# A gated recurrence with a mixture of adapters: the adapter weights issued from GpSimd instead of the sync engine

## The chip, the cores and the metric

The kernel runs on one core of a Trainium2 chip. The metric is the device time of one execution in microseconds (us), the median of several runs. A profile of one execution gives the span from the first to the last instruction; it is a little shorter than the measured time.

A core has TensorE (PE in the profile, with the loads of its stationary operand as PEld), VectorE (DVE), ScalarE (ACT), GpSimd (POOL) and a sync engine (SP) that does no arithmetic and here issues transfers. Each engine works through its own instructions in order; semaphores join them.

## The reference

For each of 4 batches and 8 heads, a recurrence over 768 steps with a 48 x 48 state, then a mixture of 8 low-rank adapters over all 3072 rows of width 384, of which each row uses two:

```python
for t in range(S):                       # S = 768, D = 48
    state = alpha[:, :, t, :, None] * state + np.einsum('bhd,bhe->bhde', k[:, :, t], v[:, :, t])
    y[:, :, t] = np.einsum('bhd,bhde->bhe', q[:, :, t], state)
...
x = y.transpose(0, 2, 1, 3).reshape(B * S, H * D)      # 3072 x 384
logits = x @ w_gate                                    # 8 experts
topk = np.argpartition(-logits, 2, axis=1)[:, :2]
w = softmax over the two chosen logits
delta[mask] += w[mask, k, None] * ((x[mask] @ A[e]) @ B[e])   # rank 16
return x + delta
```

The inputs are q, k, v, alpha of 4.7 MB each, and the small weights w_gate (384 x 8), A (8 x 384 x 16) and B (8 x 16 x 384). The output has 4.7 MB.

## The kernel before

The 768 steps of a batch are cut into 6 chunks of 128, so that there are 24 units (batch, chunk). Within a unit all 8 heads are handled together, and the recurrence becomes matrix products over a chunk plus a state carried from chunk to chunk. The stages of a unit, by the names that the code gives its functions and tiles:

- `ld` loads a whole batch of one input into a tile of 128 partitions (`a_t`, `k_t`, `q_t`, `v_t`, each 1.2 MB, two buffers each by `TURNS`).
- `ln` (ScalarE) takes the logarithm of alpha for two chunks at once into `lg`; `cum` (TensorE) forms its running sums; `eup`, `edn`, `edec` (ScalarE) take exponentials of them into `up`, `dn` and `dec`.
- `kgm`, `qgm`, `vbc` (GpSimd) multiply k by `up` into `kg`, q by `dn` into `qg`, and cast v into `vb`.
- `tr` (TensorE) transposes `kg` and `qg`; `kq` (VectorE) copies the transposes out of PSUM; `at` (TensorE) multiplies them; `msk` (VectorE) applies the causal mask into `at_sb`.
- `kv` (TensorE) and `sdm` (VectorE) carry the state, `sdec`.
- `yt` (TensorE) forms the transposed result, `xs` (ScalarE) copies it, `z` (TensorE) multiplies it by `W`, which holds A and w_gate side by side; `gmx`, `gdf`, `gex`, `gwu`, `grd`, `gzw` (VectorE, and ScalarE for the exponential) choose and weigh the two experts.
- `zt`, `qs`, `av`, `delta` (TensorE) build the output of the unit in one PSUM bank `y`, with `B_all` as the last factor; `fin` (ScalarE) copies it to `o`, and `st` stores it.

The order of all this on each engine is fixed when the kernel is built, by a planner. `graph` makes a node for each stage of each unit, with an assumed cost from `STAGES` and a priority that is the unit's number less a lead from `LEAD`; `CHAINS` and `RINGS` give the dependencies, the latter those from buffers being used again. `list_order` then places the nodes one after another on their engines, and `plan` returns them in that order; `emit` calls the function of each. The stores are placed behind the last load.

The loads stand in the order of `load_list`: alpha, k, q, v of batch 0, then an item `"w"`, which is all the weights, then the twelve loads of batches 1 to 3. All of them are issued by the sync engine (`load_engine`), so that they are in one queue. The item `"w"` is `wload`: for each half of the 128 partitions (even and odd heads of a pair, rows 0 to 47 and 64 to 111) four transfers of A, one for each pair of heads, and one of w_gate, and one transfer of B at the end; eleven in all, into the float32 tiles `W_st` and `B_st`. `wcast` then casts these on VectorE into the bfloat16 tiles `W` and `B_all`, with two copies for the halves of W and one for B:

```python
nc.vector.tensor_copy(out=W[rows], in_=W_st[rows])
...
nc.vector.tensor_copy(out=B_all, in_=B_st)
```

For the planner this cast is a node `wcast`, on which every `z` depends.

Of the kernel before, what the change touches and what calls it, by code (L numbers as in the profile page):

```python
# [13 lines left out]
F4 = mybir.dt.float32  # L14

B, H, S, D = 4, 8, 768, 48
# [3 lines left out]
E = 8  # L20
R = 16
P = 128
NP = H // 2
HP = 64
NW = E * R + E
G = 2
RING = 4
QRING = 3
VRING = 5
SRING = 4  # L30
# [8 lines left out]
def _bc_mid(src: bass.AP, reps) -> bass.AP:  # L39
# [17 lines left out]
    "st": ("DMA", 655, 2455),  # L57
}
LEAD = {
    "vld": 4.5, "vbc": -39.07, "ln": -78.94, "cum": -6.57, "edn": -64.56, "eup": 56.94,  # L60
    "edec": -16.31, "kgm": -144.25, "qgm": -36.9, "tr": 10.78, "kq": -190.71, "sdm": -68.3,
    "kv": 0.43, "at": 71.13, "msk": -50, "qs": 15.22, "av": 80.82, "xb": 0.5, "xt": 0.4,
    "xs": -65.35, "z": -58.98, "zc": -33.57, "gmx": -40, "gdf": 13.75, "gex": 14.25, "gwu": -45.2,
    "grd": 9.49, "gw": -7.12, "gzw": -43.82, "yt": -51.21, "zt": -11.39, "zs": -8.95,
    "delta": 56.73, "fin": -111.57, "st": 100,
}
CHAINS = (
    "ln cum eup kgm tr kq at msk yt xs z gmx gdf gex gwu grd gzw zt zs delta fin st",
# [1 line left out]
    "vbc yt", "zt qs av delta", "zt av",  # L70
)
RINGS = (
    ("kgm", "eup", 3), ("qgm", "edn", 3), ("sdm", "edec", 6), ("tr", "kgm", RING), ("kv", "kgm", RING),
    ("tr", "qgm", QRING), ("kv", "vbc", VRING), ("av", "vbc", VRING), ("at", "kq", 5), ("av", "kq", 5),
    ("msk", "at", 1), ("av", "msk", 4), ("z", "xs", 3), ("delta", "zs", 3), ("st", "fin", 24),
    ("qs", "sdm", SRING), ("kv", "sdm", 1), ("kgm", "cum", 3), ("qgm", "cum", 3), ("at", "tr", 5),
    ("av", "tr", 5), ("z", "yt", 3), ("delta", "zt", 3), ("st", "zt", 24),
    ("edec", "kv", -1), ("qs", "kv", SRING - 1), ("delta", "gzw", 3),
)
HOLDS = {  # L80
# [81 lines left out]
def load_list():  # L162
    out = []
    for b in range(B):
        if b in ():
            seq = [(0, 0)]
            for c in range(NCH):
                seq += [(1, c), (2, c), (0, c + 1), (3, c)]
            out += [(b, i, c) for i, c in seq if c < NCH]
        else:  # L170
            out += [(b, i, None) for i in range(4)]
    return out[:4] + ["w"] + out[4:]


def load_engine(x):
    return "ACT" if x in ((0, 1, 0), (0, 3, 0)) else "SP"


def graph(lead):
    nodes, deps = {}, []  # L180

    def has(f, u):
        c = u % NCH
        if not 0 <= u < NU or (f in ("sdm", "edec", "qs") and c == 0):
            return False
        if f == "ln" and u // NCH not in () and u % G:
            return False
        return not (f == "kv" and c == NCH - 1)

    def dep(a, b):  # L190
        if a in nodes and b in nodes:
            deps.append((a, b))

    for f in STAGES:
        for u in range(NU):
            if f != "ln2" and has(f, u):
                t = STAGES["ln2" if f == "ln" and u // NCH not in () else f]
                nodes[f, u] = t + (u - lead[f],)
    nodes["wcast", 0] = ("DVE", 700, 700, 0)
    dep(("wcast", 0), ("z", 0))  # L200
    for u in range(NU):
        for line in CHAINS:
            names = line.split()
            for f, g in zip(names, names[1:]):
                dep((f, u if has(f, u) or f != "ln" else u - 1), (g, u))
        for f, g, d in RINGS:
            dep((f, u - d), (g, u))
        dep(("kv", u - 1), ("sdm", u))
        for w in range(NU):
            if w // G == u // G - 2:  # L210
                dep(("cum", w), ("ln", u))
    for x, item in enumerate(load_list()):
        n = ("ld", x)
        eng = load_engine(item)
        if item == "w":
            nodes[n] = ("DMA", 4000, 5300, x)
            dep(n, ("wcast", 0))
            continue
        b, i, c = item
        t = 1060 if c is not None else 4450  # L220
        nodes[n] = ("DMB" if eng == "POOL" else "DMA", t, t + 1300, x)
        mine = [(READER[i], b * NCH + k) for k in (range(NCH) if c is None else (c,))]
        for m in mine:
            dep(n, m)
        if eng == "POOL":
            nodes["is", x] = ("POOL", 1000, 1000, b * NCH + (c or 0) - 6)
            deps.append((("is", x), n))
            n = ("is", x)
        if b >= TURNS[i]:
            for k in range(NCH):  # L230
                dep((READER[i], (b - TURNS[i]) * NCH + k), n)
    last = ("ld", len(load_list()) - 1 - 0)
    for u in range(NU):
        dep(last, ("st", u))
    holds = {}
    for f, readers in HOLDS.items():
        for u in range(NU):
            if (f, u) in nodes:
                holds[f, u] = [(g, u + d) for g, d in readers if (g, u + d) in nodes]
    return nodes, deps, holds  # L240
# [22 lines left out]
def kernel(  # L263
# [11 lines left out]
    nc = tc.nc  # L275
# [2 lines left out]
    loads = ctx.enter_context(tc.tile_pool(name="loads", bufs=3))  # L278
    outp = ctx.enter_context(tc.tile_pool(name="outp", bufs=24))
    consts = ctx.enter_context(tc.tile_pool(name="consts", bufs=1))  # L280
    scal = ctx.enter_context(tc.tile_pool(name="scal", bufs=3))
    trsb = ctx.enter_context(tc.tile_pool(name="trsb", bufs=5))
    atsb = ctx.enter_context(tc.tile_pool(name="atsb", bufs=4))
    moep = ctx.enter_context(tc.tile_pool(name="moep", bufs=3))
    PS = bass.MemoryType.PSUM
    ps_s = ctx.enter_context(tc.tile_pool(name="ps_s", bufs=1, space=PS))
# [13 lines left out]
    ENG = {"SP": nc.sync, "ACT": nc.scalar, "POOL": nc.gpsimd}  # L300

    def load(b, i, c, eng):
        name, src = SRC[i]
        if raw[b][i] is None:
            raw[b][i] = loads.tile([P, H * NCH, 64], F4, name=name, tag=name, bufs=TURNS[i])
            batches[b][i] = raw[b][i].rearrange("p (h c) d -> p c h d", h=H)[:, :, :, 0:D]
        if c is None:
            eng.dma_start(  # L308
                out=raw[b][i][:, :, 0:D], in_=src[b].rearrange("h (c j) d -> j (h c) d", j=C))
        else:  # L310
            eng.dma_start(
                out=batches[b][i][:, c],
                in_=src[b][:, c * C:(c + 1) * C, :].rearrange("h j d -> j h d"))

    W_st = consts.tile([P, NP, NW], F4, name="W_st")
    B_st = consts.tile([P, DM], F4, name="B_st")
    W = consts.tile([P, NP, NW], F2, name="W")
    B_all = consts.tile([P, DM], F2, name="B_all")

    def wload():  # L320
        for hh in range(2):
            rows = slice(HP * hh, HP * hh + D)
            for p in range(NP):
                f0 = (2 * p + hh) * D
                nc.sync.dma_start(  # L325
                    out=W_st[rows, p, 0:E * R].rearrange("f (e r) -> f e r", e=E),
                    in_=moe_A[:, f0:f0 + D, :].rearrange("e f r -> f e r"))
            nc.sync.dma_start(
                out=W_st[rows, :, E * R:NW],
                in_=moe_w_gate.rearrange("(p t f) e -> t f p e", p=NP, t=2)[hh])  # L330
        nc.sync.dma_start(out=B_st, in_=moe_B.rearrange("e r f -> (e r) f"))

    def wcast(_):
        for hh in range(2):
            rows = slice(HP * hh, HP * hh + D)
            nc.vector.tensor_copy(out=W[rows], in_=W_st[rows])  # L336
        nc.vector.tensor_copy(out=B_all, in_=B_st)

    items = load_list()

    def ld(x):
        if items[x] == "w":
            wload()
        else:
            load(*items[x], ENG[load_engine(items[x])])

    order = plan()[1]
    early = [n for n in order if n[0] == "ld"][:4]
    for n in early:
        ld(n[1])  # L350
# [5 lines left out]
        out=suf, in_=suf, compare_op=ALU.is_gt, fill=0.0, base=0,  # L356
# [14 lines left out]
    for i in range(2):  # L371
        t = consts.tile([P, G, H, HP], F2, name=f"lg{i}")
        nc.gpsimd.memset(t[:, :, :, D:HP], 0.0)
        lgs.append(t)
    for lst, nm, n in ((kgs, "kg", RING), (qgs, "qg", QRING), (vbs, "vb", VRING)):
        for i in range(n):
# [3 lines left out]
    for i in range(SRING):  # L380
# [8 lines left out]
        out=mask, in_=mask, compare_op=ALU.is_ge, fill=0.0, base=0,  # L389
# [4 lines left out]
    st = [dict() for _ in range(NU)]  # L394
# [46 lines left out]
    def kgm(u):  # L441
        s = st[u]
        b, c = units[u]
        s["kg"] = kgs[u % RING]
        nc.gpsimd.tensor_tensor(  # L445
# [178 lines left out]
    def store(u):  # L624
# [2 lines left out]
        nc.sync.dma_start(out=out[t0:t0 + C, :], in_=st[u]["o"])  # L627

    emit = dict(
        ld=ld, wcast=wcast, ln=ln, cum=cum, eup=eup, edn=edn, edec=edec, kgm=kgm, qgm=qgm, vbc=vbc,  # L630
        tr=tr, kq=kq, sdm=sdm, kv=kv, at=at, msk=msk, qs=qs, av=av, yt=yt, xs=xs, z=z,
        gmx=gmx, gdf=gdf, gex=gex, gwu=gwu, grd=grd, gzw=gzw, zt=zt, zs=zs, delta=delta, fin=fin,
        st=store)
# [33 lines left out]
```

## Time and profile before

| | before |
|---|---|
| measured time, median of 3 (lowest, highest) | 111.11 us (111.11, 111.3) |
| span of the profiled execution | 110.4 us |
| mean granted TensorE clock | 0.956 of full speed |
| TensorE busy | 79.6 us (72%) |
| VectorE busy | 76.0 us (69%) |
| ScalarE busy | 64.3 us (58%) |
| GpSimd busy | 61.9 us (56%) |
| moved by the DMA engines | 24.21 MB, 219 GB/s on average |

In the lines of the profile, `out<-in` names the tiles by the program's names, a line number such as L325 is one of the kernel's code, and `xN` counts instructions. The idle time before a group and what ended it stand at the end of a line. SPq is the time in which the sync engine's queue issues transfers; a transfer moves on after its issue, so its landing has to be read from those that wait for it. Busy times of engines overlap each other and do not add up to the span.

### The profile page before, as it was taken

The numbers are of one execution on the slowest core, as the hardware profiler recorded it, in microseconds if no ns is written. First come the engines' busy times: TensorE is split into PE (matmuls) and PEld (weight loads), VectorE is DVE, ScalarE is ACT, GpSimd is POOL, SyncE is SP. The second block draws the span as 40 slices with busy tenths as digits, with TensorE's granted clock in tenths as the row PEclk, the third lists the DMA queues.
The fourth block names the chain that finished last, engine by engine and source line by source line (L and its number), as shares of the span: only waits on it lengthen the run. The fifth ranks groups of instructions, "written<-read, shape, count | busy, mean of one in ns | idle before, by whom it ended". The sixth has DMA issues, their size and how long they took to land.

```text
span 110.4 us, 3341 instructions
## 1 busy us (share of the span) xinstructions
PE 79.6 (72%) x1312; PEld 61.0 (55%) x1312; DVE 76.0 (69%) x227; ACT 64.3 (58%) x177; POOL 61.9 (56%) x97
## 2 busy tenths in 40 slices
PE   0005206981896959988599999999939998997850
PEld 0003105761775747876486777776727976865720
DVE  4000002989976597799797979999947699999810
ACT  4029402542028997693979559967955367563560
POOL 7600649999001185899575949983749749500000
PEclk9999999999769999999999999999996799999995
DMA  0979899533889898996979989785959899441052
GB/s 19 307 219 297 236 281 291 96 35 83 222 230 296 214 299 242 250 287 187 320 229 278 283 236 290 198 243 146 286 143 308 324 391 356 145 175 39 6 207 78
DMA packets 32064, 24.21 MB, mean 219 GB/s; under 512 B 4272, under 2 KB 32048, under 8 KB 32048
## 3 DMA queue, kind: packets, MB, share of 16 engines
q1 hardware_dynamic: 32048, 24.00, 73.8%
q8 instruction: 10, 0.16, 0.6%
q14 instruction: 6, 0.05, 0.1%
HBM read 19.28 MB, written 4.72 MB: 217 GB/s over the span
## 4 chain that ended last, share of the span: by engine, by line
SPq 30%; DMA 27%; PE 22%; ACT 11%; issue 3%; DVE 3%; POOL 1%; ACTq 0%
SPq L308 21%; DMA a_t<-in_alpha_dram 16%; DMA q_t<-in_q_dram 11%; SPq L325 8%; PE tr L477 4%; ACT xs L539 4%; PE y L615 3%; ACT lg L402 3%; PE at L507 2%; PE yt L531 2%; PE yt L526 2%; PE y L554 2%; PE z L562 2%; ACT o L622 1%; ACT up L426 1%
## 5 line engine op out<-in xcount | busy, mean ns | idle before, releaser
L445 POOL TENSOR_TENSOR kg<-k_t,up 128x384 bf16<-128x384 f32 x24 | 23.9, 1011 | 14.6 <-DMA k_t<-in_k_dram 9.9
L515 DVE TENSOR_TENSOR at_sb<-at,mask 128x1024 bf16<-128x1024 f32 x24 | 29.2, 1217 | 4.1 <-PE at L507 3.9
L483 DVE COPY kq<-tr 128x1024 bf16<-128x1024 bf16 x24 | 16.2, 683 | 19.5 <-PE tr L477 19.3
L452 POOL TENSOR_TENSOR qg<-q_t,dn 128x384 bf16<-128x384 f32 x24 | 23.6, 1001 | 6.4 <-DMA q_t<-in_q_dram 6.1
L459 POOL CAST vb<-v_t 128x384 bf16<-128x384 f32 x24 | 11.6, 508 | 12.7 <-PE y L554 10.4
L539 ACT CAST xs<-yt 128x512 bf16<-128x512 f32 x24 | 14.2, 599 | 6.6 <-PE yt L531 6.4
L426 ACT ACTIVATE up<-cum 128x384 f32<-128x384 f32 x24 | 11.1, 492 | 9.2 <-PE cum L417 9.0
L411 PE MATMUL cum<-lg,suf 128*128 128x384 bf16 x24 | 8.6, 368 | 8.7 <-ACT lg L402 8.7
L622 ACT COPY o<-y 128x384 f32<-128x384 f32 x24 | 11.4, 481 | 5.3 <-PE y L615 5.3
L477 PE MATMUL tr<-ident,qg 128*128 128x128 bf16 x96 | 10.6, 241 | 5.4 <-POOL qg L452 5.4
L402 ACT ACTIVATE lg<-a_t 128x768 bf16<-128x768 f32 x12 | 10.1, 847 | 7.2 <-DMA a_t<-in_alpha_dram 7.2
L477 PE MATMUL tr<-ident,kg 128*128 128x128 bf16 x96 | 10.6, 241 | 3.3 <-POOL kg L445 3.3
L562 PE MATMUL z<-W,xs 128*128 128x136 bf16 x96 | 9.2, 225 | 4.4 <-DVE W L336 2.7
L464 DVE TENSOR_TENSOR sdec<-kv,dec 128x384 bf16<-128x384 f32 x20 | 10.9, 547 | 1.8 <-PE kv L497 1.8
L431 ACT ACTIVATE dn<-cum 128x384 f32<-128x384 f32 x24 | 11.5, 523 | 0.0
L611 ACT CAST zs<-y 128x128 bf16<-128x128 f32 x24 | 6.4, 266 | 7.9 <-PE y L554 7.4
L477 PEld LDWEIGHTS <-qg 128*128 128x128 bf16 x96 | 7.4, 110 | 5.8 <-POOL qg L452 5.8
L531 PE MATMUL yt<-at_sb,vb 128*64 128x128 bf16 x192 | 10.2, 228 | 0.6 <-DVE at_sb L515 0.5
L507 PE MATMUL at<-kq 48*128 48x128 bf16 x192 | 10.2, 229 | 0.5 <-DVE at_sb L515 0.4
L615 PE MATMUL y<-B_all,zs 128*128 128x384 bf16 x24 | 8.0, 341 | 2.3 <-ACT zs L611 1.5
L562 PEld LDWEIGHTS <-xs 128*128 128x128 bf16 x96 | 5.7, 98 | 6.4 <-ACT xs L539 3.5
L477 PEld LDWEIGHTS <-kg 128*128 128x128 bf16 x96 | 6.6, 106 | 4.7 <-POOL kg L445 3.4
(53 smaller groups left out, 148.9 us busy)
## 6 DMA issues: line engine op xcount, KB each, us to landing
out_dram<-o SPq DMA_DIRECT2D x24, 192.0 KB, 2.7
W_st<-in_moe_A_dram SPq DMA_DIRECT2D x8, 24.0 KB, 2.7
B_st<-in_moe_B_dram SPq DMA_DIRECT2D x1, 192.0 KB, 2.4
a_t<-in_alpha_dram SPq DMA_DIRECT2D x4, 0.2 KB, 8.8
k_t<-in_k_dram SPq DMA_DIRECT2D x4, 0.2 KB, 10.7
q_t<-in_q_dram SPq DMA_DIRECT2D x4, 0.2 KB, 9.9
v_t<-in_v_dram SPq DMA_DIRECT2D x4, 0.2 KB, 9.8
W_st<-in_moe_w_gate_dram SPq DMA_DIRECT2D x2, 6.0 KB, 1.9
```

What stands on the lines that cost most here:

```text
L308: eng.dma_start(out=raw[b][i][:, :, 0:D], in_=src[b].rearrange("h (c j) d -> j (h c) d", j=C))
L402: nc.scalar.activation(lgs[(u // G) % 2][:, :, :, 0:D], batches[b][0][:, c:c + G], AF.Ln)
L445: nc.gpsimd.tensor_tensor(out=s["kg"][:, :, 0:D], in0=batches[b][1][:, c], in1=s["up"], op=ALU.mult)
L452: nc.gpsimd.tensor_tensor(out=s["qg"][:, :, 0:D], in0=batches[b][2][:, c], in1=s["dn"], op=ALU.mult)
L477: nc.tensor.transpose(t[:, w, p, :], pair(src, p), ident[:, :])
L483: nc.vector.tensor_copy(out=s["kq"], in_=s["tr"])
L507: nc.tensor.matmul(t[:, hh, p, :], s["kq"][rows, 0, p, :], s["kq"][rows, 1, p, :], start=True, stop=True)
L515: nc.vector.tensor_tensor(out=s["at_sb"].rearrange("p a b t -> p (a b) t"), in0=s["at"].rearrange("p a b t -> p (a b) t"), in1=_bc_mid(mas ...
L531: nc.tensor.matmul(s["yt"][HP * hh:HP * hh + HP, p, :], s["vb"][:, 2 * p + hh, :], s["at_sb"][:, hh, p, :], start=(c == 0 and p == 0), sto ...
L539: nc.scalar.copy(s["xs"], s["yt"])
L562: nc.tensor.matmul(s["z"], s["xs"][:, p, :], W[:, p, :], start=(p == 0), stop=(p == NP - 1))
L622: nc.scalar.copy(s["o"], s["y"])
```

## The change

The weights leave the queue of the sync engine. The item `"w"` is gone from `load_list`, and `wload` is a node of its own on GpSimd, ahead of everything else there. It has five DMAs instead of eleven: for each half of the partitions one of A, with the four pairs of heads and the eight experts merged into one access pattern, and one of w_gate, and one of B. For this the columns of `W_st` are laid out as (expert, pair, rank) with the gate's columns behind them, and `wcast` puts them into their places in W, with two copies for each half and one for B, on VectorE. The node `wcast` now depends on `wload`.

In the order that the planner makes of it, the five casts stand on VectorE directly behind the memsets of the set-up and ahead of the first `kq`. In the kernel before they stand behind the third `at_sb`.

With this, five kinds of buffers get one more: `kg` (`RING` 4 to 5), `up` and `dn` (the pool `scal` 3 to 4), `kq` (the pool `trsb` 5 to 6) and `at_sb` (the pool `atsb` 4 to 5), with the numbers in `RINGS` to match, and `LEAD` has new values, which change the order of the work on all engines. On ScalarE, for one, `dn` now mostly comes ahead of `up`. The copy of the transposes, `kq`, is a VectorE instruction in both kernels.

```diff
-RING = 4
+RING = 5
...
-    return out[:4] + ["w"] + out[4:]
+    return out
...
-    nodes["wcast", 0] = ("DVE", 700, 700, 0)
+    nodes["wload", 0] = ("POOL", 8000, 13000, -99)
+    nodes["wcast", 0] = ("DVE", 1600, 1700, 99)
+    dep(("wload", 0), ("wcast", 0))
...
-    scal = ctx.enter_context(tc.tile_pool(name="scal", bufs=3))
-    trsb = ctx.enter_context(tc.tile_pool(name="trsb", bufs=5))
-    atsb = ctx.enter_context(tc.tile_pool(name="atsb", bufs=4))
+    scal = ctx.enter_context(tc.tile_pool(name="scal", bufs=4))
+    trsb = ctx.enter_context(tc.tile_pool(name="trsb", bufs=6))
+    atsb = ctx.enter_context(tc.tile_pool(name="atsb", bufs=5))
...
-    W_st = consts.tile([P, NP, NW], F4, name="W_st")
+    W_st = consts.tile([P, NP * NW], F4, name="W_st")
...
-    def wload():
+    def wload(_):
         for hh in range(2):
             rows = slice(HP * hh, HP * hh + D)
-            for p in range(NP):
-                f0 = (2 * p + hh) * D
-                nc.sync.dma_start(
-                    out=W_st[rows, p, 0:E * R].rearrange("f (e r) -> f e r", e=E),
-                    in_=moe_A[:, f0:f0 + D, :].rearrange("e f r -> f e r"))
-            nc.sync.dma_start(
-                out=W_st[rows, :, E * R:NW],
+            nc.gpsimd.dma_start(
+                out=W_st[rows, 0:E * NP * R].rearrange("f (x r) -> f x r", r=R),
+                in_=bass.AP(tensor=moe_A.tensor, offset=moe_A.offset + hh * D * R,
+                            ap=[[R, D], [2 * D * R, E * NP], [1, R]]))
+            nc.gpsimd.dma_start(
+                out=W_st[rows, E * NP * R:].rearrange("f (p e) -> f p e", p=NP),
                 in_=moe_w_gate.rearrange("(p t f) e -> t f p e", p=NP, t=2)[hh])
-        nc.sync.dma_start(out=B_st, in_=moe_B.rearrange("e r f -> (e r) f"))
+        nc.gpsimd.dma_start(out=B_st, in_=moe_B.rearrange("e r f -> (e r) f"))
 
     def wcast(_):
         for hh in range(2):
             rows = slice(HP * hh, HP * hh + D)
-            nc.vector.tensor_copy(out=W[rows], in_=W_st[rows])
-        nc.vector.tensor_copy(out=B_all, in_=B_st)
+            nc.vector.tensor_copy(
+                W[rows, :, 0:E * R].rearrange("f p (e r) -> f e p r", e=E),
+                W_st[rows, 0:E * NP * R].rearrange("f (e p r) -> f e p r", e=E, p=NP))
+            nc.vector.tensor_copy(
+                W[rows, :, E * R:NW], W_st[rows, E * NP * R:].rearrange("f (p e) -> f p e", p=NP))
+        nc.vector.tensor_copy(B_all, B_st)
```

## The prediction

> **What bounds the kernel now.** I read four views of the kernel before, in this order: the chain of work that ended last, the sync engine's queue in order of time, the busy time of the engines by stretches, and the waits. The chain first, since it says what kind of thing the end hangs on:
>
> ```profile
> SPq 30%; DMA 27%; PE 22%; ACT 11%; issue 3%; DVE 3%; POOL 1%; ACTq 0%
> SPq L308 21%; DMA a_t<-in_alpha_dram 16%; DMA q_t<-in_q_dram 11%; SPq L325 8%; PE tr L477 4%; ACT xs L539 4%; PE y L615 3%; ACT lg L402 3%; PE at L507 2%; PE yt L531 2%; PE yt L526 2%; PE y L554 2%; PE z L562 2%; ACT o L622 1%; ACT up L426 1%
> ```
>
> SPq is the queue that issues the loads, DMA the flight of a load. Together they are 57% of the chain: the end hangs on when the big loads arrive, and 8% (8.8 us of 110.4) is one line, L325, the small weight loads. The queue in order of time (start, duration, then the transfer) shows where those sit:
>
> ```profile
> 11.14 3.89 SPq L308 DMA_DIRECT2D v_t<-in_v_dram  x1
> 15.08 5.84 SPq L325 DMA_DIRECT2D W_st<-in_moe_A_dram  x4
> ...
> 21.48 3.28 SPq L325 DMA_DIRECT2D W_st<-in_moe_A_dram  x4
> ...
> 25.32 0.44 SPq L331 DMA_DIRECT2D B_st<-in_moe_B_dram  x1
> 25.97 0.70 SPq L308 DMA_DIRECT2D a_t<-in_alpha_dram  x1
> 27.12 4.85 SPq L308 DMA_DIRECT2D k_t<-in_k_dram  x1
> ```
>
> The last load of batch 0 is issued by 15.03, the first of batch 1 only at 25.97: eleven small issues hold the queue for 10.9 us, some 4 us of which is waiting behind the loads already queued (the first of L325 takes 4.29), the rest 0.44 to 0.47 us each and one of 1.76. The stretches (after the length: busy time of PE, PEld, DVE, ACT, POOL with counts, the granted clock, the DMA engines' busy share, GB/s) show what this does to the transfers:
>
> ```profile
> 16.00:20.00 4.00, 2.49 (x27) 1.93 (x28) 1.23 (x2) 0.94 (x3) 3.54 (x4) 1.00 0.95 284
> 20.00:22.00 2.00, 2.00 (x26) 1.65 (x27) 1.89 (x3) 1.09 (x4) 2.00 (x4) 1.00 0.49 53
> 22.00:24.00 2.00, 1.74 (x36) 1.30 (x30) 1.71 (x3) 1.33 (x4) 2.00 (x4) 1.00 0.44 47
> 24.00:26.00 2.00, 1.15 (x21) 0.84 (x18) 2.00 (x4) 0.64 (x2) 2.00 (x4) 1.00 0.18 16
> ```
>
> From 20 to 26 us the DMA engines are busy 0.98 + 0.88 + 0.36 = 2.2 us of 6 and move next to nothing. The waits (engine, line, released by: total us, times, longest) and VectorE in order of time show who pays:
>
> ```profile
> DVE kq L483 <- PE tr L477: 19.3, 5, 15.8
> POOL kg L445 <- DMA k_t<-in_k_dram: 9.9, 2, 7.4
> PE z L562 <- DVE W L336: 2.7, 1, 2.7
> ```
>
> ```profile
> 18.16 0.69 DVE L483 COPY kq<-tr 128x1024 bf16<-128x1024 bf16 x1 [15.81 <-PE tr L477]
> ...
> 25.74 0.97 DVE L336 CAST W<-W_st 48x544 bf16<-48x544 f32 x1
> 26.90 0.96 DVE L336 CAST W<-W_st 48x544 bf16<-48x544 f32 x1 [0.20 <-DMA W_st<-in_moe_w_gate_dram]
> 27.89 0.36 DVE L337 CAST B_all<-B_st 128x384 bf16<-128x384 f32 x1
> ...
> 44.65 1.43 DVE L483 COPY kq<-tr 128x1024 bf16<-128x1024 bf16 x2 [0.66 <-PE tr L477]
> ...
> 83.13 0.69 DVE L483 COPY kq<-tr 128x1024 bf16<-128x1024 bf16 x1 [1.69 <-PE tr L477]
> ```
>
> VectorE starts real work at 18.16 and is busy for 76.0 us in all, 1.2 of it before. From 18.2 on, its idle time is about 12 us before its work ends near 105. Some 3.7 us of that lie between 34 and 46 (8.29 us busy of 12), where batch 1 has not arrived, and 3.3 between 78 and 90 (8.70 of 12), around the late q_t and v_t of batch 3. Elsewhere it runs at 94 to 98% (66 to 78 us: 11.7 of 12). So there are two bounds close together: late loads, and behind them VectorE, with TensorE (79.6 us busy) near it.
>
> [...] what the weights cost is 10.9 us of queue, but only 2.2 us of engine time, so only the first can vanish. [...] The trace has no GpSimd DMA at all.
>
> **The change part by part.**
> - *Weight loads leave the sync queue.* The load of a_t of batch 1 can be issued at 15.08 instead of 25.97. It then waits for room as the first weight load does (4.29). Landings follow each other at about 4.45 us when nothing is between (k_t to q_t of batch 1: consumers at 38.16 and 42.61). v_t of batch 0 lands at about 20.8 and a_t of batch 1 at 33.3, 12.5 us apart, so 8.0 us are the gap. The weights' 2.2 to 2.4 us of engine time do not vanish: they move among the loads of batch 0. Net: every load from batch 1 on lands about 5.6 us earlier, q_t of batch 3 at 76.0 instead of 81.6. The buffers allow it: k_t of batch 2, say, would be issued near 40, and its buffer's last reader is done at 27.6.
> - *Five DMAs on GpSimd.* They stand behind the set-up (ending 4.74) and ahead of the first kg, for which GpSimd idles 7.40 us anyway, till 12.14. Behind them are four kg (0.95 apart) and qg, which needs q_t (16.46). [...] I take 8, just hidden.
> - *When the weights land.* The bytes and the 3,456 small rows are the same as before; merged DMAs save issues, not rows. [...] Upper, if packets alternate with those of the loads: (3,456 + 128) / 16 = 224 packets for each DMA engine, each about 10 ns (2.2 us / 224) beside a load packet of about 45 ns (4.4 us for 96): 224 × 55 ns = 12.3, from 5 to 6 us on, so 17.5 to 18.5. I take 18.5, since the queue of the loads is never empty then.
> - *Casts at the head of VectorE.* The order of the changed kernel puts five copies ahead of the first kq, so all of VectorE's work waits for the last weight. Two large copies (48x512 instead of 48x544, at most 0.97), two of 32 columns (about 0.1 each, as the small memsets) and B_all (0.36) are 2.4 us. First kq at 18.5 + 2.4 = 20.9 instead of 18.16: **2.7 us later**. q_t itself may be 2.3 later, which alone would give 20.5, so the two overlap.
> - *Casts leave the middle.* VectorE's 2.5 us from 25.74 to 28.25, and PE's 2.69 wait for W, go: **2.5 us gained**.
> - *Batch 1 is there in time.* q_t at about 37.0 instead of 42.6, while VectorE would come to the end of batch 0's work at about 41: **3.7 us gained**.
> - *Batch 3.* VectorE arrives 3.5 us earlier (2.7 − 2.5 − 3.7), at 81.4 − 3.5 = 77.9; q_t at 76.0 plus 1.0 (qg) and 0.4 (transposes) is 77.5. The wait of 1.69 closes, and about 1.0 of the smaller ones up to 90: **2.7 us gained**.
> - *One more buffer each of kg, up, dn, kq and at_sb, and new leads.* These change the order everywhere; no single row prices that. I count nothing, since VectorE at 94 to 98% in full stretches leaves little to a better order; both signs stay in the range. The transposes' copy stays on VectorE in the code (0.68 each).
>
> Sum: 2.7 − 2.5 − 3.7 − 2.7 = −6.2. Span 110.4 − 6.2 = 104.2; the measured time stands 0.7 above the span (111.1 against 110.4), so **104.9 us**.
>
> **The rivals.**
> - *Better still: VectorE packs tightly.* From 20.9, its remaining 76.0 − 1.2 − 2.3 = 72.5 us at 95%, plus the 4.9 us that follow its last work now: 20.9 + 76.3 + 4.9 = 102.1, so 102.8. For it: stretches of 94 to 98% exist, and buffers get deeper. Against it: the end of the kernel has too few chunks to fill (98 to 106 us: 6.6 of 8).
> - *The earlier loads buy little, and TensorE or the new order becomes the bound.* TensorE is at 3.7 to 3.9 us of 4 in most stretches from 42 on. If only the gap of batch 1 (3.7) is gained and the start's 2.7 against the casts' 2.5 stay: 110.4 − 3.5 = 106.9; with a reshuffle costing another 1 to 2, about 108.5 + 0.7 = 109.
> - *A new wait in place of the old one, slower.* If [...] the weights land at 28, kq starts at 30.4 and everything queued behind it on VectorE shifts: 104.2 + 9.5 + 0.7 = 114.4. GpSimd's kg and qg then wait too. The break-even is a landing near 25. For it: no trace here shows a GpSimd DMA, and an in-order VectorE stands behind it. [...]
>
> **How the numbers follow.** My forecast 0.45, tighter packing 0.22, little gained 0.18, weights late 0.15. All but the last, and a sliver of the third, are faster: faster 0.83, same 0.02, slower 0.15. The range reaches from just under the tight case (101.0) to just under no gain (111.0); it leaves out most of the late case and a very tight one, together about 0.2.
>
> **What would show it.** Right: a_t of batch 1 issued at about 15 and its logarithm near 28; DMA busy share above 0.8 from 16 to 30; the casts ending by 21 and the first kq right after; no wait of VectorE over 1 us between 25 and 90; the DMA share of the chain well under 57%. Wrong: GpSimd's first kg after 16, or casts after 25; a first kq that waits for the casts more than 4 us; batch 1 on time, but VectorE and TensorE with as much idle time as before.

## The result, and the profile after

| | before | after |
|---|---|---|
| measured time, median of 4 (lowest, highest) | 111.17 us (111.11, 111.3) | 108.31 us (106.74, 111.13) |
| ratio after / before, 95% interval | | 0.9635 (0.9573 to 0.9698) |
| span of the profiled execution | 110.4 us | 109.4 us |
| VectorE busy, TensorE busy | 76.0, 79.6 us | 75.3, 77.9 us |
| mean granted TensorE clock | 0.956 | 0.975 |

The changed kernel is faster by 3.65%, which is 4.1 us of 111.17; the medians lie 2.9 us apart. The forecast was 6.2. Ratios here and below leave disturbed runs out, so they are not the quotients of the medians. A second profile of the changed kernel is called "again" below; its span is 107.4 us, 3.0 less than before. None of the profiled executions is a short one: they took 112.17 us (before), 111.13 (after) and 109.18 (again), while the shortest of the changed kernel took 106.7.

The chain of work that ended last, of the kernel after:

```profile
SPq 34%; DMA 29%; PE 13%; POOL 8%; DVE 8%; ACT 3%; issue 3%; ACTq 0%; POOLq 0%
```

The weights' line is gone from it, and yet queue and flight of the loads have 63% where they had 57% (again, 54%): the prediction's sign "well under 57%" did not appear. The sync engine's queue in order of time (start, duration, transfer):

```profile
12.93 5.41 SPq L306 DMA_DIRECT2D v_t<-in_v_dram  x1
18.79 3.83 SPq L306 DMA_DIRECT2D a_t<-in_alpha_dram  x1
23.07 4.31 SPq L306 DMA_DIRECT2D k_t<-in_k_dram  x1
27.82 5.39 SPq L306 DMA_DIRECT2D q_t<-in_q_dram  x1
...
38.18 5.93 SPq L306 DMA_DIRECT2D a_t<-in_alpha_dram  x1
```

a_t of batch 1 is issued at 18.79 instead of 25.97, so the gap of 10.9 us has closed. But v_t of batch 0 is now issued by 18.34 instead of 15.03. GpSimd in order of time shows the new issues, and who waits:

```profile
4.85 1.11 POOL L321 DMA_DIRECT2D W_st<-in_moe_A_dram  x1
...
8.07 0.57 POOL L328 DMA_DIRECT2D B_st<-in_moe_B_dram  x1
16.39 3.86 POOL L443 TENSOR_TENSOR kg<-k_t,up 128x384 bf16<-128x384 f32 x4 [7.75 <-DMA k_t<-in_k_dram]
20.20 3.87 POOL L450 TENSOR_TENSOR qg<-q_t,dn 128x384 bf16<-128x384 f32 x4
```

The five issues run from 4.85 to 8.64, 3.8 us in all. Then GpSimd waits 7.75 us for k_t: the first kg starts at 16.39, where it was 12.14, and the first qg, behind four kg, at 20.20, where it was 16.46. A first kg after 16 is one of the prediction's signs of being wrong; again, it starts at 14.51. VectorE in order of time:

```profile
15.26 0.42 DVE L333 CAST W<-W_st 48x512 bf16<-48x512 f32 x1 [5.15 <-DMA W_st<-in_moe_A_dram]
...
16.05 0.36 DVE L338 CAST B_all<-B_st 128x384 bf16<-128x384 f32 x1 [0.27 <-DMA B_st<-in_moe_B_dram]
21.90 0.69 DVE L481 COPY kq<-tr 128x1024 bf16<-128x1024 bf16 x1 [5.49 <-PE tr L475]
```

The casts are done by 16.4, and then VectorE waits 5.49 us more for the transposes. So the first kq is late (21.90 against 18.16), but not because of the casts. The stretches (length; busy time of PE, PEld, DVE, ACT, POOL; clock; DMA share; GB/s), to be read against those of before:

```profile
16.00:20.00 4.00, 0.61 (x4) 0.34 (x4) 0.36 (x1) 0.00 (x0) 3.61 (x4) 1.00 0.69 198
20.00:22.00 2.00, 0.74 (x6) 0.57 (x7) 0.10 (x1) 0.00 (x0) 2.00 (x3) 1.00 1.00 297
22.00:24.00 2.00, 2.00 (x24) 1.44 (x23) 1.39 (x3) 0.94 (x3) 2.00 (x3) 1.00 0.87 241
24.00:26.00 2.00, 2.00 (x30) 1.82 (x28) 1.89 (x3) 0.94 (x3) 2.00 (x5) 1.00 0.91 272
...
42.00:46.00 4.00, 2.38 (x46) 1.86 (x43) 3.31 (x6) 2.80 (x10) 2.09 (x4) 1.00 0.46 112
```

From 20 to 26 us the DMA engines are busy 5.6 us of 6, where they were 2.2. But from 16 to 20 the core almost stands (PE 0.61 of 4, before 2.49). And a new thin stretch has come in at 42 to 46, at 112 GB/s, under the long issue of a_t that begins at 38.18.

At batch 3, GpSimd and then VectorE:

```profile
78.15 1.96 POOL L450 TENSOR_TENSOR qg<-q_t,dn 128x384 bf16<-128x384 f32 x2 [2.26 <-DMA q_t<-in_q_dram]
```

```profile
79.64 0.69 DVE L481 COPY kq<-tr 128x1024 bf16<-128x1024 bf16 x1 [1.69 <-PE tr L475]
```

q_t of batch 3 is there at 78.15 (again, 77.70), earlier than the 81.64 of before, but later than the 76.0 of the forecast. The wait of 1.69 us at 83.13, which the forecast had closing, has only moved: it is 1.69 us at 79.64 (again, 1.82 at 79.19).

To part the start from the rest I use the time from the first kq to the end of the span: 110.4 − 18.16 = 92.2 us before, 87.5 after and 87.3 again. The start costs 3.7 us (again, 2.0: first kq at 20.13), and the rest gains 4.7 to 4.9. In five experiments below whose GpSimd begins in the same way (e1, e11, e15, e17, e18) the first kq comes at 19.92 to 20.79, so 1.8 to 2.6 us is the usual cost of the start, and 3.7 that of one long execution.

### The profile page after: what moved, and what is told of

Same layout as the page of the kernel before. It is cut to its first block, busy times and chain, and to the rows that moved or that the text cites. A ratio compares the mean times of both kernels' runs of the same rounds, so it can differ in the third digit from the quotient of the medians.

```text
span 109.4 us, 3347 instructions
## 1 busy us (share of the span) xinstructions
PE 77.9 (71%) x1312; PEld 59.2 (54%) x1312; DVE 75.3 (69%) x229; ACT 63.5 (58%) x177; POOL 65.5 (60%) x103
## 4 chain that ended last, share of the span: by engine, by line
SPq 34%; DMA 29%; PE 13%; POOL 8%; DVE 8%; ACT 3%; issue 3%; ACTq 0%; POOLq 0%
SPq L306 34%; DMA v_t<-in_v_dram 20%; DMA q_t<-in_q_dram 10%; POOL vb L457 4%; POOL qg L450 3%; DVE kq L481 2%; DVE at_sb L513 2%; PE tr L475 2%; PE y L613 2%; DVE sdec L462 1%; PE yt L529 1%; PE z L560 1%; PE y L543 1%; PE y L552 1%; PE at L505 1%
## 5 line engine op out<-in xcount | busy, mean ns | idle before, releaser
L475 PE MATMUL tr<-ident,qg 128*128 128x128 bf16 x96 | 10.1, 231 | 4.1 <-POOL qg L450 4.1
L560 PE MATMUL z<-W,xs 128*128 128x136 bf16 x96 | 9.8, 227 | 0.8 <-ACT xs L537 0.6
L475 PEld LDWEIGHTS <-qg 128*128 128x128 bf16 x96 | 6.9, 105 | 4.7 <-POOL qg L450 4.7
L333 DVE CAST W<-W_st 48x512 bf16<-48x512 f32 x2 | 0.8, 422 | 12.3 <-DMA W_st<-in_moe_A_dram 12.3
## 6 DMA issues: line engine op xcount, KB each, us to landing
q_t<-in_q_dram SPq DMA_DIRECT2D x4, 0.2 KB, 10.9
```

What stands on the lines that cost most here:

```text
L475: nc.tensor.transpose(t[:, w, p, :], pair(src, p), ident[:, :])
```

## The experiments

My theory: the gain is the freed queue plus the casts' removal from the middle, less a later start. Rivals: the casts' place is what counts, not the queue; the new leads and buffers bring it; merging eleven DMAs into five would do, from any queue. The runs were made in three groups. The kernel before, beside them, took 113.15 us in the first (110.79 to 113.96), 112.39 in the second (111.04 to 113.66) and 112.48 in the third (110.5 to 113.72), medians of 7; the first group gave no ratio with an interval. Between groups, ratios to the kernel before can be compared, and times only roughly.

### One part alone, planned anew

**Weights on GpSimd alone (e1).** The kernel before with the change's `wload`, `wcast` and nodes, and the old leads and buffers:

```diff
-    return out[:4] + ["w"] + out[4:]
+    return out
...
-    nodes["wcast", 0] = ("DVE", 700, 700, 0)
+    nodes["wload", 0] = ("POOL", 8000, 13000, -99)
+    nodes["wcast", 0] = ("DVE", 1600, 1700, 99)
...
+            nc.gpsimd.dma_start(
```

> The kernel before with the weights issued from GpSimd in five DMAs, and nothing else: its leads and buffer counts are kept. If the gain comes from taking the weights out of the queue of the loads, this run has most of the change's 4.0 us: 106.5 to 108.5. If the new leads and the extra buffers bring it, this run stays within 1 us of 111.2.

Measured: 112.09 us (110.72 to 112.96), no gain outside the spread. Yet the last load was issued by 74.81 instead of 80.29, and the first kq came at 20.03. So the loads were 5.5 us earlier, and the time did not follow.

**Leads and buffers alone (e2).** The kernel after with the weights as before, in eleven DMAs of the sync engine:

```diff
-    return out
+    return out[:4] + ["w"] + out[4:]
...
-            nc.gpsimd.dma_start(
+            for p in range(NP):
...
+                nc.sync.dma_start(
```

> The changed kernel with the weights issued from the sync engine in eleven DMAs as before; the new leads and the extra buffers are kept. If the queue is the cause, this run stays within 1 us of 111.2, with the first load of batch 1 issued near 26. If the order and the buffers are, it has the change's time, about 107.

Measured: 119.46 us (117.82 to 120.63), slower than either theory allowed.

**No weights at all (e6).** The kernel after without the loads of w_gate, A and B; it computes with zero weights:

```diff
     def wload(_):
-        for hh in range(2):
...
+        nc.gpsimd.memset(W_st, 0.0)
+        nc.gpsimd.memset(B_st, 0.0)
```

> The changed kernel with no weight loads at all: GpSimd fills the two staging tiles with zeros, so the adapter part of the result is left out, while all its arithmetic still runs. If the late start of VectorE (21.90 instead of 18.16) is the weights' transfers standing among the loads of batch 0, the first kq is back near 18 to 18.5 and the time is about 3.5 us below the changed kernel's, 103.5 to 104.5. If the four kg ahead of the first qg are the cause, the first kq stays near 21 and the time near 107.

Measured: 106.52 us (104.74 to 108.83), span 103.0. GpSimd, and then VectorE, in order of time:

```profile
12.08 3.86 POOL L435 TENSOR_TENSOR kg<-k_t,up 128x384 bf16<-128x384 f32 x4 [6.33 <-ACT up L416]
```

```profile
17.99 0.69 DVE L473 COPY kq<-tr 128x1024 bf16<-128x1024 bf16 x1 [10.96 <-PE tr L467]
```

kg no longer waits for k_t and is back at 12.08, kq at 17.99: without the weights' transfers the late start is gone. In the kernel after they are under way between 4.85 and about 16 us, as k_t is, with the DMA engines busy throughout (share 1.01 from 4 to 16 us). (The five issues are gone with them, but those ended at 8.64, before k_t had landed.) In the table of DMA queues of the kernel after they take only 2.6% of 109.4 = 2.8 us, as a mean over the DMA engines. The time, though, is 2 to 3 us above the 103.5 to 104.5 that was expected.

**Five merged DMAs on the sync engine (e7),** at the old place in the queue:

```diff
-            nc.gpsimd.dma_start(
+            nc.sync.dma_start(
...
-    return out
+    return out[:4] + ["w"] + out[4:]
```

> The changed kernel with its five merged DMAs issued from the sync engine, between the loads of batch 0 and batch 1, where the eleven stood; leads and buffers of the changed kernel. If the number of issues was the cost and not their engine, the queue is held about 4.3 + 4 x 0.5 = 6.5 us instead of 10.9, batch 1 is issued near 22, the start stays at 18.2, and the time is 106 to 108. If any weight transfer in this queue drains the DMA engines, it is near 110 to 111.

Measured: 114.14 us (111.77 to 115.5), no gain. The five still held the queue from 15.64 to 22.65, 7.0 us for 10.9. The planner made yet another order here, so this doesn't price the 3.9 us saved.

What follows from the group: parts planned anew can't be compared. Each edit changed the order on all engines, and that can move the time by more than the edit: compare e2 with e10, and e1 with e17, below, each beside its own time of the kernel before. So from here the order is held: taken from one of the two kernels, with the items of the weights alone moved by hand.

### One part alone, in a kept order

**The order of after, weights on the sync engine (e10),** behind batch 0 in eleven DMAs, casts just ahead of the first z:

```diff
     for n in early:
         ld(n[1])
+    wload(0)
...
+        if n == ("z", 0):
+            wcast(0)
-        if n not in early:
+        if n not in early and n[0] not in ("wload", "wcast"):
```

> The changed kernel's order on every engine kept as it is, but the weights issued from the sync engine in eleven DMAs behind batch 0, as before, and the casts moved on VectorE to just ahead of the first z. If the queue is what the change gains on, with the order equal, this is 3 to 6 us slower than the changed kernel although its start is 3.7 us earlier: batch 1 issued near 26. If the order alone carries the gain, it is as fast as the changed kernel or faster by its earlier start.

Measured: 113.73 us (113.08 to 115.42), ratio 1.013 (0.9975 to 1.0285). With the weights in the old queue, the new leads and buffers bring nothing. The kernel after in the same group (below) has 0.956 (0.9413 to 0.9706), clear of this interval and 5.6 us less, as the first expectation had it. And nearly the same parts as in e2, in another order, take 5.7 us less, of which 0.8 lies between the two groups.

**The order of before, weights from GpSimd (e11),** the casts at their old place:

```diff
-            wload()
+            pass
...
+    wload(0)
```

> The order of the kernel before kept as it is on every engine, casts included, with only the weights issued from GpSimd in five DMAs at the head. The prediction's arithmetic was made for just this: the loads from batch 1 on 5.6 us earlier and the gaps closed, so 5 us less than before. If an order fits only the arrival times it was planned for, it gains at most 2 us, as the run with old leads and a new plan did.

Measured: 109.5 us (109.1 to 110.18), ratio 0.9799 (0.9697 to 0.99). The queue alone, with the merging of eleven DMAs into five, brings 2.0%, about 2.2 us. The last load was issued by 73.49, 6.8 us earlier than before: more than three times what the time gained. Its chain shows why no more came of it:

```profile
PE 46%; DVE 18%; ACT 13%; DMA 10%; SPq 5%; issue 3%; POOL 1%; ACTq 0%; DVEq 0%; POOLq 0%
```

Queue and flight of the loads are 15% of it, where they were 57%: the loads are no longer what the end hangs on, and TensorE and VectorE are.

**The order of after, casts just ahead of the first z (e15),** weights from GpSimd:

```diff
+        if n == ("z", 0):
+            wcast(0)
-        if n not in early:
+        if n not in early and n[0] != "wcast":
```

> The changed kernel with one thing moved: the five casts stand on VectorE just ahead of the first z instead of at the head. If casts in a stretch where GpSimd multiplies cost 3.7 us, this is 2 to 4 us slower than the changed kernel: ratio to before 0.975 to 0.995. If the cast's place does not matter, 0.955 to 0.965.

Measured: 110.15 us (109.22 to 110.99), ratio 0.984 (0.9675 to 1.0005), against 0.9635 with the casts at the head. VectorE in order of time, and the wait that follows:

```profile
26.54 1.20 DVE L333 CAST W<-W_st 48x512 bf16<-48x512 f32 x1
27.66 0.96 DVE L336 CAST W<-W_st 48x32 bf16<-48x32 f32 x1
28.65 1.17 DVE L333 CAST W<-W_st 48x512 bf16<-48x512 f32 x1
29.74 0.17 DVE L336 CAST W<-W_st 48x32 bf16<-48x32 f32 x1
```

```profile
PE z L560 <- DVE W L336: 3.7, 1, 3.7
```

The same copies that took 0.42 and 0.17 us at the head take up to 1.20 and 0.96 here, and z waits for them. The stretches of this kernel show a second cost:

```profile
26.00:30.00 4.00, 0.33 (x5) 0.21 (x4) 3.94 (x6) 0.50 (x1) 3.13 (x4) 0.95 0.88 241
30.00:34.00 4.00, 4.00 (x41) 2.53 (x40) 3.42 (x12) 1.93 (x4) 0.00 (x0) 0.50 0.57 153
```

While z waits, TensorE is busy for 0.33 us of 4, and in the 4 us after that its clock is 0.50. In the kernel before the wait was 2.69 us, with the same sequel:

```profile
28.50:29.00 0.50, 0.48 (x10) 0.29 (x5) 0.50 (x3) 0.00 (x0) 0.00 (x0) 1.00 1.00 290
29.00:29.50 0.50, 0.47 (x5) 0.35 (x5) 0.50 (x3) 0.21 (x1) 0.00 (x0) 0.61 0.92 247
...
31.50:32.00 0.50, 0.50 (x7) 0.28 (x4) 0.09 (x2) 0.34 (x1) 0.00 (x0) 0.50 0.83 240
...
33.00:34.00 1.00, 0.49 (x5) 0.28 (x4) 1.00 (x3) 0.65 (x1) 0.00 (x0) 1.00 0.91 247
```

For some 3 us the clock is about 0.50. From 22 to 34 us the kernel after has 1.00 throughout.

**The order of before, casts first (e17).** The kernel before with the weights from GpSimd and the casts at the head of VectorE, with the old leads and buffers:

```diff
-            wload()
+            pass
...
+    wload(0)
...
+    wcast(0)
     for n in order:
-        if n not in early:
+        if n not in early and n[0] != "wcast":
```

> The order of the kernel before on every engine, weights from GpSimd, and the casts at the head of VectorE: all of the change but the leads and the extra buffers. If issue engine and place of the casts are the change, it has its whole gain, ratio 0.955 to 0.965. If the new leads or the buffers carry a part, it stays at 0.97 to 0.98, as the run with the casts in their old place.

Measured: 106.68 us (106.08 to 107.88), ratio 0.9572 (0.945 to 0.9694): the whole gain, and the lowest median but for the kernel without weights, though its interval overlaps that of after. Against the same order with the casts in the middle (0.9799) it is lower by 2.3%, some 2.5 us; the two were run in different groups, and their intervals just part. Its VectorE in order of time:

```profile
8.95 0.42 DVE L335 CAST W<-W_st 48x512 bf16<-48x512 f32 x1 [6.59 <-DMA W_st<-in_moe_A_dram]
...
14.12 1.16 DVE L335 CAST W<-W_st 48x512 bf16<-48x512 f32 x1 [4.67 <-DMA W_st<-in_moe_A_dram]
15.20 0.97 DVE L338 CAST W<-W_st 48x32 bf16<-48x32 f32 x1
16.20 1.10 DVE L340 CAST B_all<-B_st 128x384 bf16<-128x384 f32 x1
20.02 0.69 DVE L487 COPY kq<-tr 128x1024 bf16<-128x1024 bf16 x1 [2.72 <-PE tr L481]
```

and its GpSimd:

```profile
14.00 3.08 POOL L449 TENSOR_TENSOR kg<-k_t,up 128x384 bf16<-128x384 f32 x3 [5.54 <-DMA k_t<-in_k_dram]
```

At 8.95, with GpSimd idle, the large copy takes 0.42 us; at 14.12, beside kg, the same copy takes 1.16. Here too VectorE waits for the transposes afterwards (2.72 us), so that these slow casts delay no kq. Later VectorE has no wait over 0.71 us between 44 and 90 us: the one at batch 3 is gone. Queue and flight are 16% of the chain, and the clock is 1.00 in every stretch. This profile is of its longest execution, 107.88 us.

**The same with the five extra buffers (e18),** order unchanged:

```diff
-RING = 4
+RING = 5
...
-    scal = ctx.enter_context(tc.tile_pool(name="scal", bufs=3))
+    scal = ctx.enter_context(tc.tile_pool(name="scal", bufs=4))
```

and `trsb` and `atsb` likewise.

> The run before this one with the five extra buffers, order unchanged. If the buffers let engines run ahead, it is 0.5 to 2 us below that one; if they only serve the planner, it has its time within 0.5 us.

Measured: 108.83 us (107.6 to 110.52), ratio 0.9746 (0.9599 to 0.9893). No gain from the buffers: the median is 2.2 us above e17, which neither expectation allowed. Whether they cost something, the overlapping intervals don't tell.

**The kernel after once more,** beside the kept orders:

> The changed kernel itself, as the measure for the three kernels beside it on the same chip: 3 to 4% below the kernel before.

Measured: 108.13 us (106.72 to 110.55), ratio 0.956 (0.9413 to 0.9706), as the first time.

### Sparing k_t

**Weights from ScalarE's queue (e12),** meant to be issued behind the third logarithm, casts ahead of the first z, order of after:

```diff
-            nc.gpsimd.dma_start(
+            nc.scalar.dma_start(
...
+        if n == ("z", 0):
+            wcast(0)
...
+        if n == ("ln", 4):
+            wload(0)
```

> The changed kernel's order kept; the five DMAs go to ScalarE's queue behind its third logarithm, near 13.6 us, where ScalarE idles till 22, and the casts on VectorE to just ahead of the first z. k_t then lands before any weight moves. If the late start is the weights ahead of k_t, the first kq is at 18 to 19.5 instead of 21.9 and the time 1.5 to 3 us below the changed kernel's, less 1.5 us of casts that now lie in VectorE's busy stretch: 0.5 to 2 us faster. If it is the engine of the issue, nothing changes.

Measured: 109.81 us (109.28 to 110.32), ratio 0.982 (0.9716 to 0.9924), first kq at 19.40. The queue did not wait for the logarithm: the weights were issued from 10.78, while that logarithm ran at 12.74. So k_t was spared (first kg at 12.42), but q_t paid: the first qg came at 17.70, 1.2 us later than before. z waited 4.1 us for the casts, and the clock was 0.51 from 26 to 30 us and 0.64 from 30 to 34. The ratio is that of e15 (0.984), whose casts stand in the same place and whose first kq is 1.3 us later, at 20.68.

**The same with the casts on ScalarE (e13),** in three pieces behind two `up` and one `xs`:

```diff
-            nc.vector.tensor_copy(
...
+        nc.scalar.copy(
...
+    CAST_AT = {("eup", 4): 0, ("eup", 5): 1, ("xs", 0): 2}
```

> As the run with the weights on ScalarE's queue, but the casts are also ScalarE's, in three parts between its exponentials, so that VectorE has none. If that run lost what it gained by its casts beside GpSimd's products (3.7 us on VectorE, and 4.1 us in which z waited), this one starts at 19.4 without that loss and is 1.5 to 3 us below the changed kernel: ratio to before 0.93 to 0.945. If the kernel is bound later whatever its start is, the ratio stays at 0.95 to 0.965.

Measured: 109.03 us (108.2 to 110.02), ratio 0.9776 (0.9625 to 0.9927), first kq at 20.16: a miss. The weights were issued at the same early time, so the late start was not cured, and the try tells nothing of a really later issue.

## Why the prediction was right, and where its sizes were off

The forecast of 104.9 us was 3.4 us below the median of 108.31; its range held it, and the side was right. What was read of before, a queue held for 10.9 us while the DMA engines drain, is what the gain comes from: in the order of after, leaving the weights in that queue gives 1.013, taking them out 0.984, and with the casts at the head 0.9635; in the order of before the same two steps give 0.9799 and 0.9572. The intervals of neighbouring steps touch or nearly do; first and last of each row lie clear of each other.

That the sum fell into the range is in part luck, for most of its signs did not come: a_t of batch 1 was issued at 18.79 (again, 17.40) and not at about 15, the DMA share from 16 to 20 was 0.69, the first kq did not follow right after the casts, VectorE waits over 1 us at 46.43 and 79.64, and the chain kept its loads. One reading was wrong without harm: the measured time does not stand 0.7 above the span, since the profiled execution of before took 112.17 us, 1.8 above its span of 110.4 (after: 1.7). The 104.9 is the same as 111.1 less 6.2, so it stands.

- *Issue on GpSimd.* Forecast 8 us, just hidden; measured 3.8, hidden behind the wait for k_t. The 8 was an estimate of the room in the profile of before, not of the issues: 16.46 for the first qg, less 3.8 for four kg and the 4.7 at which the set-up ends. One issue holds GpSimd for 0.57 to 1.11 us here.
- *Landing of the weights and casts at the head.* Forecast 18.5 and then 2.4 us of casts; measured about 16 and 1.54 (again, 3.06, the last two of them beside the first kg). That the weights' packets alternate with those of the loads was the author's assumption, which no run shows. The casts never held the first kq.
- *Start.* Forecast 2.7 us later; measured 3.7 and, again, 2.0. The size is near, the cause another: k_t is late when the weights move with it, and four kg stand ahead of the first qg. The prediction named "q_t itself may be 2.3 later" as the lesser of two causes; it left out that k_t would be later still (kg 4.2 us, again 2.4).
- *Casts leave the middle.* Forecast 2.5 us; e11 against e17 gives 2.3%, about 2.5, and e15 against after 2.1%, with intervals that overlap. But it isn't only VectorE's own time: part of it is copies that take longer while GpSimd multiplies (1.20 us for 0.42 in e15), and behind the wait of z the clock falls to 0.50 (for some 3 us in before), which the prediction didn't count.
- *The gaps of batches 1 and 3.* This is the step that failed in size. "Every load from batch 1 on lands about 5.6 us earlier" became 3.7 us by the end of the last issue (76.63 against 80.29; again, 4.2), and between k_t of batch 2 and q_t of batch 3 the issues are only 1.4 to 2.0 us earlier (again, 2.1 to 2.7), since batch 0 is issued later and two issues last 5.39 and 5.93 us. VectorE's busy time between 34 and 46 us rose from 8.30 to 10.43 us (again, 9.58), and between 78 and 90 from 8.70 to 9.11 (again, 9.87): 2.5 us of the 6.4 forecast, in both profiles. "The wait of 1.69 closes" did not come true in the order of after; in e17 it did, and VectorE is busy for 11.32 us between 78 and 90.
- *Leads and buffers.* Counted as nothing; in the kept orders nothing is what they show (e17 has neither). But that held only for this order: see e2.

So the sum: 2.0 to 3.7 for the start, 2.5 for the casts (from e11 and e17, not from these profiles) and 2.5 for the gaps, where the forecast had 2.7, 2.5 and 6.4. That makes 1.3 to 3.0 us of gain, near what the spans of the two profiles have (1.0 and 3.0). The ratio's 4.1 is more than either, because it is of shorter executions of the changed kernel, of which none was profiled. From the first kq on, 4.7 to 4.9 us were gained instead of 8.9. Even loads that come in time don't give their whole lead back: in e11 they are 6.8 us earlier and the time falls by 2.2. The prediction held late loads to be the first bound and VectorE the one close behind; it then forecast the gain as if the second were far off.

Five things stay open. Why some issues of big loads take 5.3 to 6.5 us instead of about 4.1, with thin transfers under them, was not tried; it comes in most of these kernels, before among them (5.29 us at 69.32), at changing places. Nor was a way found to issue the weights after k_t and q_t. Whether five merged DMAs in the sync engine's queue would do, in a kept order, was not run. How much of the gain is the clock's is not parted: in before it also fell to 0.72 and 0.86 from 82 to 86 and 86 to 90 us, in e17 nowhere; but one execution of before, in the third group, had a mean of 0.997 and still took 111.23 us, so it is not the whole. And the first four runs of after spread from 106.7 to 111.1 us; a late start of 3.7 us in one profile and 2.0 in another is part of that, but what decides it is not shown.

## What to carry to other kernels

The small transfers in the queue of the big loads cost 10.9 us of its time here, for 2.2 us of work of the DMA engines: give such transfers another issuer, but look at which first load is then under way with them, for here that one, k_t, came later (first kg by 4.2 us, again 2.4). Set-up copies belong where their engine waits anyway, ahead of their consumer: in the middle they cost themselves and a consumer's wait (2.69 us in before, 3.7 in e15), and the clock fell to 0.50 after it. Where a planner lays the order, hold it fixed when a part is tested: the same weights on GpSimd and casts at the head gave 112.09 us planned anew and 106.68 in the old order (the kernel before beside them: 113.15 and 112.48).

## What the runs showed of the hardware

- VectorE's float32 to bfloat16 copies of the weights take longer while GpSimd multiplies: 48x512 takes 0.42 us with GpSimd idle and up to 1.20 beside its products (e15), 48x32 takes 0.17 and 0.97 (e17), 128x384 takes 0.36 (after) and 1.10 (e17). One product takes about 0.97 (kg in after: 3.86 us for four).
- The granted clock fell to 0.50 after TensorE had waited for the casts: after a wait of 2.69 us in before, of 1.9 in e11 (0.63 as the mean from 30 to 34 us) and of 3.7 in e15. Not every idle stretch had this sequel: in after TensorE was busy for 0.61 us of the four from 16 to 20, and the clock stayed at 1.00 to 34 us.
- In e12 a DMA in ScalarE's queue was issued at 10.78 us, before a logarithm that stands ahead of it in the program had run (12.74), so that what is said ahead of engines working in order does not extend to these issues.
- For the same 0.41 MB of weights the profile counts 224 packets in GpSimd's queue (after) and 3,664 in the queue that ScalarE issues into (e12), where the forecast of the landing had 224 for each DMA engine and took the rows to be the same; but the time on the DMA engines is alike: 2.6% of 109.4 = 2.8 us in after and 2.8% of 107.7 = 3.0 us in e12.
